# Two attentions in a row: the first one's weights are divided by their sums before they are transposed

## The chip, the core and the metric

The kernel runs on one NeuronCore of a Trainium2 chip, as one launch. Its time is the device time of one execution in microseconds (us). Every kernel is executed several times; the median is given with the lowest and the highest run. One execution is also recorded by the hardware profiler: it has a time of its own, and a span, from its first recorded instruction to its last.

## The reference

Two layers of attention stand behind each other: batch 8, 576 rows, 8 heads of width 64 first, and then 4 experts with one causal head of width 64 each, of which each row takes the best two.

```python
scores = scale * q @ k.T                                # first attention, per batch and head: 576 x 576
scores = np.where(scores >= max(scores) - tau, scores, -1e9)
a = exp(scores - max(scores)); a /= a.sum() + 1e-9
x = a @ v                                               # heads side by side: 576 x 512
for e in range(4):                                      # second attention, causal
    q, k, v = x @ wq[e], x @ wk[e], x @ wv[e]
    s = where(causal, -1e9, scale * q @ k.T)
    p = exp(s - max(s)); p /= p.sum() + 1e-9
    out += gate[e] * (p @ v @ wo[e])                    # the gate is a softmax over the best two
```

## The kernel before

The 64 (batch, head) pairs are worked as 32 pairs of heads, `n` = 0 to 31, four to a batch. Each pair's 576 query rows are cut into four tiles of 128 rows and a tail of 64. `scores(n, s)` (lines 331 to 361) makes one tile `s`: the matmuls of queries and keys, split in a high and a low part, go to PSUM (L1087 for every matmul); DVE copies the scores to SBUF and takes their minimum (they are negated) in one instruction (`s_min`, L1177); ACT takes the exponential (`s_exp`, L1190); DVE compares the scores with the threshold, multiplies the exponentials with the outcome and sums each row (`s_stt`, L1194: the threshold product of the text below). There are two such rows of 576 per tile, one per head, and one for the tail, where both heads share the 128 partitions: 288 for the whole kernel. TensorE then transposes the weights (`tr_pp`, L1239), and ACT or DVE evacuates them to `pa` and `pt` (L1063, L1065).

`attnv(n, tiles)` (lines 363 to 393) multiplies the transposed weights with `v`, in two groups of tiles per pair, 64 in all. The weights are not normalised at that point. The row sums were collected in a buffer `sg`; `g_sum` adds the epsilon (L1058), `g_inv` inverts (L1202), `g_wide` and `g_tail` spread each inverse over 64 columns in `iw` (on POOL L1067, on ACT L1063, on DVE L1065), TensorE transposes `iw` (`tr_inv`, by the helper at L1077), ACT or DVE evacuates that to `iv`, and DVE multiplies it with the product that lies in PSUM (`x_mul`, L1277; `x_tail`, L1281). `x_hi` and `x_lo` split the outcome in two parts for the second attention, which begins with projections that read `x`.

`second(b)` (from line 415) is the second attention of one batch. It divides its weights by their sums before their transposes: `add_eps` (L1058), `inv` (L1230), `share` for the gate (L1235) and `scale2` (L1492 on POOL and DVE, L1490 on ACT).

Two tables write the order out by hand. `ORDER` gives each task a place in one long list, `BY` gives its engine where it has a choice, and `plan` (from line 157) walks the list and gives out the buffers: eight `e` buffers for scores and weights, eight banks of PSUM, in pairs for transposes (class `d`) and scores (class `s`). Each engine runs its instructions in the order of the list and waits by semaphores for what the others make; TensorE has no choice of engine, and what comes next on it is what the list says.

```python
def evac(n, fn, deps, takes=(), uses=(), name="", engs=("ACT", "DVE")):   # out of PSUM
def small(fn, deps, sm, name):                                            # DVE, ACT or POOL
def scale2(self, e, sm, p2, w, j):
    p, x = self.row(p2)[:, :w], self.small(sm)[:, 10 + j:11 + j]
```

Of the kernel before, what the change touches and what calls it, by code (L numbers as in the profile page):

```python
# [246 lines left out]
def work(K):  # L247
# [47 lines left out]
    LD, PREP, PTS, VMB, X, AV, SUMS = {}, {}, {}, {}, {}, {}, {}  # L295
# [1288 lines left out]
```

## Time and profile before

| | |
|---|---|
| median of 3 runs | 832.75 us (831.75 to 833.85) |
| the profiled execution | 832.69 us, span 831.0 us |
| TensorE (PE), weight loads (PEld) | 808.6 us busy, 763.1 us busy |
| VectorE (DVE) | 733.6 us busy |
| ScalarE (ACT) | 653.5 us busy |
| GpSimd (POOL) | 280.9 us busy |

The busy time of an engine is the time in which at least one of its instructions runs; a line's share of it is counted so that overlapped time isn't counted twice. A matmul's end is modelled, so a busy PE need not work at its peak pace. "Idle before" is time for which an engine stood still ahead of a group's instructions, with what ended most of it. A line number can be that of a helper, so that the names of the tiles (out<-in) tell which step it is: `ps<-ident,iw` is the transpose of the inverse sums, `ps<-ident,e` at L1239 that of the first attention's weights.

### The profile page before, as it was taken

The page shows a single profiled execution, that of the slowest core. Times are in us where ns is not written, and L with a number is a line of the kernel's source. Part 1 is how long each engine was busy: PE and PEld are TensorE (multiplying, and loading weights), DVE is VectorE, ACT ScalarE, POOL GpSimd, SP SyncE. Part 2 cuts the span into 40 slices and gives each one's busy share as a digit, 9 for nine tenths or more (in the row PEclk, how much of TensorE's full clock was granted, in tenths as well). Part 3 has the DMA queues.
Part 4 walks back from the last instruction along what each step waited for, and adds up shares of the span by engine and source line. Part 5 has one row for each costly group of instructions (what it writes and reads, how often), then busy time and mean ns, then how long its engine had stood idle before and what let it go on. Part 6 is the DMA issues. An engine that isn't in the chain of part 4 may idle for free.

```text
span 831.0 us, 35075 instructions
## 1 busy us (share of the span) xinstructions
PE 808.6 (97%) x14472; PEld 763.1 (92%) x14472; DVE 733.6 (88%) x2327; ACT 653.5 (79%) x1374; POOL 280.9 (34%) x604
## 2 busy tenths in 40 slices
PE   9989999999999999999999999999999999989998
PEld 7888999999989998899999999989998899988997
DVE  6999999998899889899988999998999988889474
ACT  4999779976898679887689767898679877779465
POOL 5756504412332124521235231521133422231451
PEclk9999999999999999999999999999999999999999
DMA  4433212122121212122112321113022113110002
GB/s 108 97 85 79 51 35 47 32 61 50 30 69 44 79 44 46 33 52 46 30 44 63 90 70 30 39 32 97 22 60 60 27 55 76 33 40 3 15 27 78
DMA packets 135632, 43.18 MB, mean 52 GB/s; under 512 B 130608, under 2 KB 130608, under 8 KB 135472
## 3 DMA queue, kind: packets, MB, share of 16 engines
q1 hardware_dynamic: 134240, 40.64, 20.1%
q8 instruction: 114, 1.87, 1.0%
q10 hardware_dynamic: 1232, 0.30, 0.2%
q14 instruction: 46, 0.38, 0.2%
HBM read 31.47 MB, written 9.44 MB: 49 GB/s over the span
## 4 chain that ended last, share of the span: by engine, by line
PE 75%; DVE 14%; ACT 7%; issue 3%; SPq 1%; DMA 1%; POOL 0%; DVEq 0%; ACTq 0%; POOLq 0%
PE ps L1087 61%; PE ps L1239 7%; PE ps L1077 6%; DVE e L1194 4%; DVE e L1177 4%; ACT pt L1063 2%; ACT e L1190 1%; DVE e L1464 1%; ACT e L1469 1%; SPq L1090 1%; DVE kk L1134 1%; DVE iv L1277 1%; ACT pa L1063 1%; DMA qi<-in_q_dram 0%; DVE pt L1065 0%
## 5 line engine op out<-in xcount | busy, mean ns | idle before, releaser
L1190 ACT ACTIVATE e<-e,sm 128x576 f32<-128x576 f32 x288 | 214.4, 770 | 24.0 <-DVE e L1177 23.2
L1177 DVE TENSOR_SCALAR_CACHE_REDUCE e<-ps 128x576 f32<-128x576 f32 x288 | 209.5, 752 | 21.4 <-PE ps L1087 16.6
L1194 DVE SCALAR_TENSOR_TENSOR e<-e,sm,e 128x576 f32<-128x576 f32 x256 | 204.7, 818 | 4.3 <-ACT e L1190 2.6
L1087 PE MATMUL ps<-kk,qq 64*128 64x288 f32 x1920 | 175.4, 306 | 3.1 <-DVE e L1177 1.8
L1063 ACT ACTIVATE pt<-ps 128x640 f32<-128x640 f32 (+3 forms) x234 | 146.5, 644 | 27.1 <-PE ps L1239 19.0
L1087 PE MATMUL ps<-pt,vm 128*64 128x128 f32 (+1 forms) x1536 | 155.9, 258 | 0.0
L1087 PEld LDWEIGHTS ps<-kk,qq 64*128 64x128 f32 x1920 | 141.2, 186 | 9.0 <-DVE e L1177 3.5
L1087 PE MATMUL ps<-pa,vm 128*64 128x128 f32 x1024 | 135.8, 276 | 1.0 <-DVE kk L1134 0.5
L1087 PEld LDWEIGHTS ps<-pt,vm 128*64 128x64 f32 x1536 | 131.1, 137 | 0.0
L1239 PE MATMUL ps<-ident,e 64*128 64x64 f32 x2624 | 124.2, 226 | 4.9 <-DVE e L1177 2.3
L1239 PEld LDWEIGHTS ps<-ident,e 64*128 64x128 f32 x2624 | 107.8, 139 | 14.9 <-DVE e L1177 4.3
L1087 PEld LDWEIGHTS ps<-pa,vm 128*64 128x64 f32 x1024 | 111.9, 137 | 6.1 <-DVE kk L1134 0.7
L1087 PE MATMUL ps<-x,wh 64*128 64x288 f32 x1024 | 106.6, 296 | 0.3 <-ACT pa L1063 0.2
L1087 PEld LDWEIGHTS ps<-x,wh 64*128 64x128 f32 x1024 | 86.1, 185 | 1.1 <-DVE e L1177 0.4
L1063 ACT ACTIVATE pa<-ps 128x512 f32<-128x512 f32 x114 | 67.0, 594 | 21.7 <-PE ps L1239 18.8
L1087 PE MATMUL ps<-x,wl 64*128 64x288 f32 x512 | 80.2, 292 | 0.0
L1492 POOL TENSOR_SCALAR e<-e,sm 128x384 f32<-128x384 f32 (+4 forms) x104 | 62.0, 604 | 36.8 <-DVE sm L1235 23.6
L1469 ACT ACTIVATE e<-e,sm 128x128 f32<-128x128 f32 (+3 forms) x128 | 70.8, 556 | 3.2 <-DVE sm L1464 2.8
L1464 DVE CUSTOM_DVE_ANT_0 e<-ps,tri 128x128 f32<-128x128 f32 (+3 forms) x128 | 58.7, 484 | 5.2 <-PE ps L1087 4.6
L1087 PE MATMUL ps<-wh,x 64*128 64x260 f32 x576 | 60.8, 285 | 0.0
L1071 POOL TENSOR_TENSOR x<-iv,x 128x64 fp32r<-128x64 f32 (+2 forms) x67 | 44.8, 678 | 41.9 <-ACT x L1063 27.9
L1087 PE MATMUL ps<-pt,vt 128*64 128x128 f32 (+1 forms) x640 | 58.9, 262 | 0.0
(163 smaller groups left out, 1650.2 us busy)
## 6 DMA issues: line engine op xcount, KB each, us to landing
vm<-in_v_dram SPq DMA_DIRECT2D x64, 128.0 KB, 2.6
out_dram<-ob SPq DMA_DIRECT2D x32, 256.0 KB, 2.4
ki<-in_k_dram SPq DMA_DIRECT2D x96, 64.0 KB, 2.4
qi<-in_q_dram SPq DMA_DIRECT2D x62, 80.0 KB, 2.4
ki<-in_k_dram SPq DMA_DIRECT2D x32, 80.0 KB, 2.5
vt<-in_v_dram SPq DMA_DIRECT2D x128, 16.0 KB, 2.1
qi<-in_q_dram SPq DMA_DIRECT2D x31, 64.0 KB, 2.3
qi<-in_q_dram SPq DMA_DIRECT2D x31, 48.0 KB, 2.5
```

Source lines behind the costliest of these rows:

```text
L1063: self.nc.scalar.activation(dst, src, AF.Copy)
L1071: eng.tensor_tensor(dst, a, b.bitcast(F32), op=ALU.subtract)
L1077: self.nc.tensor.transpose(self.ps[:, bank, c * n:(c + 1) * n], x[sl], self.ident[sl, sl])
L1087: return self.nc.tensor.matmul(out, x, y, start=first, stop=last)
L1090: (self.nc.sync if e == "SP" else self.nc.scalar).dma_start(dst, src)
L1177: self.nc.vector.tensor_scalar(self.sides(sc), self.dbank(s)[:, :, :HS], 0.0, None, op0=ALU.add, op1=ALU.min, accum_out=self.small(sm)[:, ...
L1190: self.nc.scalar.activation(self.row(e), self.row(sc), AF.Exp, bias=self.small(sm)[:, 2 * j:2 * j + 1], scale=-1.0)
L1194: self.nc.vector.scalar_tensor_tensor(self.row(e), self.row(sc), self.small(sm)[:, 8 + j:9 + j], self.row(e), op0=ALU.is_le, op1=ALU.mult, ...
L1239: self.nc.tensor.transpose(self.ps[:, g.slot + h, c * D:(c + 1) * D], x, self.ident[sl, sl])
L1464: self.nc.vector.tensor_tensor_reduce(self.row(p2)[:, :w], self.dbank(g)[:, j, :w], self.tri[:, SM - w:], 1.0, FAR, op0=ALU.add, op1=ALU.m ...
L1469: self.nc.scalar.activation(p, p, AF.Exp, bias=m[:, 2 * j:2 * j + 1], scale=-1.0, accum_out=m[:, 4 + 2 * j:5 + 2 * j])
L1492: (self.nc.vector if e == "DVE" else self.nc.gpsimd).tensor_scalar(p, p, x, 0.0, op0=ALU.mult, op1=ALU.add)
```

## The change

The row sums of the first attention stay beside the other small numbers of a tile (`sm`) and `sg`, `iw` and all that was made of them go. Behind the threshold products of a tile there are now one addition of the epsilon (`plus`, 160 of them, on DVE, ACT or POOL), one inverse (`inv`, 160, DVE) and one scaling of each row of weights in place (`scale2`, 288, on POOL, DVE or ACT), and only then the transposes. Behind the product with `v`, a plain copy out of PSUM (`x_raw`, ACT or DVE, 64) takes the place of the two products. The order tables were written anew for the new list of tasks.

```diff
-        sg, done = SUMS[n, group(s)]
-        takes = [*bufs, *dict.fromkeys((sc, ee)), sm, sg]
+        takes = [*bufs, *dict.fromkeys((sc, ee)), sm]
...
+        a = small(lambda e: K.plus(e, sm, 10, 4, nj), xs, sm, f"eps1.{n}.{s}")
+        r = task("DVE", SMALL, lambda: K.inv(sm, nj), [a], [], [sm], name=f"rec1.{n}.{s}")
+        ns = [scaling(S, lambda e, j=j: K.scale2(e, sm, ees[j], S, j), r, sm, ee, f"pn.{n}.{s}") for j in range(nj)]
-            t = pe(nc * TR + TX, lambda j=j, g=g, nc=nc: K.tr_pp(g, ees[j], nc, s < R), xs if j == nj - 1 else [x], [g, pt], [ee], "R", ld=76.0, kind="T", name=f"tm.{n}.{s}")
+            t = pe(nc * TR + TX, lambda j=j, g=g, nc=nc: K.tr_pp(g, ees[j], nc, s < R), ns if j == nj - 1 else ns[:1], [g, pt], [ee], "R", ld=76.0, kind="T", name=f"tm.{n}.{s}")
...
-        a = task("DVE", SMALL, lambda: K.g_sum(sg, nt + nm), done, [], [sg], name=f"sum.{n}.{first}")
-        r = task("DVE", SMALL, lambda: K.g_inv(sg, nt + nm), [a], [], [sg], name=f"inv.{n}.{first}")
-        u = [moved(nm * P, lambda e: K.g_wide(e, sg, iw, nm), [r], [iw], [sg, iw], name=f"iw.{n}.{first}")]
-        if tail:
-            u.append(moved(P, lambda e: K.g_tail(e, sg, iw, nm), [r], [iw], [sg, iw], name=f"iw.{n}.{first}"))
-        t = pe(nt * TR + TX, lambda: K.tr_inv(gi, iw, nt), u, [gi, iv], [iw], "R", ld=76.0, kind="T", name=f"ti.{n}.{first}")
-        i = evac(nt * P, lambda e: K.iv_out(e, iv, gi, nt), [t], [], [gi, iv], name=f"iv.{n}.{first}")
-        l = task("DVE", t_dve(w), lambda: K.x_mul(g, iv, w), [av, i], [], [g, iv], name=f"xm.{n}.{first}")
-        if tail:
-            l = task("DVE", t_dve(ST + 100), lambda: K.x_tail(g, iv, w), [l], [], [g, iv], name=f"xm.{n}.{first}")
+        l = evac(w, lambda e: K.x_raw(e, g, iv, w), [av], [iv], [g, iv], name=f"xr.{n}.{first}")
...
+    def scaling(w, fn, r, sm, buf, name):
+        x = task(None, {"POOL": (270 + 0.84 * w, 30), "DVE": (215 + 0.515 * w, 80), "ACT": (285 + 0.84 * w, 101)}, fn, [r], [], [sm, buf], name=name)
...
+    "eps1": "1222220222020002110020212212212222222020010101021212202121001222010222222222200001222020020200220000012101202022222021202020001022002120022120011222221220101200",
+    "pn": "202200220202020020201220002000220022120202011002020020022020000020000000220012110200022022122000000020000002002222002120002000200002000000200002000002002200220011202000002222020020020202220002002122000000000002200002000022202220020000002000000020002022020102220201020220100000000102000022",
```

In the table `eps1` the digits stand for DVE, ACT and POOL: 54, 28 and 78 of the additions. In `pn` they stand for POOL, DVE and ACT: 174, 16 and 98 of the scalings. Of the 64 copies of `x_raw` ACT has 45 and DVE 19.

On PE, in the middle of the program, these are the rows from the keys' transposes of one pair of heads on (`ki`: keys, `qi`: queries, `e`: weights, `kk` with `qq`: scores, `iw`: spread inverses), before:

```order
L1077 MATMUL ps<-ident,ki_76 128x64 x10
L1239 MATMUL ps<-ident,e_435_6630 128x64 x10
L1087 MATMUL ps<-kk_421_6347,qq_428_6509 128x288 x12
L1077 MATMUL ps<-ident,iw_464_7019 128x64 x6
L1077 MATMUL ps<-ident,qi_77 128x64 x10
L1087 MATMUL ps<-k_419_6283,q_415_6250 128x256 x6
```

and in the changed kernel, from the same transposes on:

```order
L1068 MATMUL ps<-ident,ki_76 128x64 x10
L1205 MATMUL ps<-ident,e_402_6428 128x64 x8
L1205 MATMUL ps<-ident,e_408_6592 128x64 x10
L1205 MATMUL ps<-ident,e_425_6840 128x64 x10
L1078 MATMUL ps<-kk_399_6369,qq_407_6572 128x288 x12
L1205 MATMUL ps<-ident,e_425_6840 128x64 x8
L1078 MATMUL ps<-k_412_6658,q2d_89 128x288 x6
```

The group `ps<-ident,iw` that stood between the scores and the queries' transposes has gone, and transposes and scores follow each other directly; at this place the scores stand somewhat further on.

On ACT, in the opening, these rows stand ahead of the second batch of head pairs before (`e<-e,sm` at L1190: exponentials; `iw`, `iv`: the inverses; `wh`: a weight of the second attention):

```order
L1190 ACTIVATE e_54_838<-e_54_838,sm 128x576
L1190 ACTIVATE e_72_1038<-e_64_941,sm 128x576
L1190 ACTIVATE e_74_1073<-e_71_1020,sm 128x576
L1063 ACTIVATE iw_75_1075<-sg 128x256
L1190 ACTIVATE e_72_1038<-e_64_941,sm 128x576
L1190 ACTIVATE e_76_1085<-e_73_1040,sm 128x576 x2
L1190 ACTIVATE e_74_1073<-e_71_1020,sm 128x576
L1124 ACTIVATE pt_77_1140<-ps,qsc 128x640
L1063 ACTIVATE iv_79_1146<-ps 128x256
```

and in the changed kernel at about the same place (L1181: exponentials; L1452: scalings; L1054: copies):

```order
L1181 ACTIVATE e_67_1059<-e_59_943,sm 128x576 x2
L1181 ACTIVATE e_69_1101<-e_66_1030,sm 128x576
L1452 ACTIVATE e_57_911<-e_57_911,sm 128x576
L1452 ACTIVATE e_51_866<-e_51_866,sm 128x576
L1181 ACTIVATE e_70_1111<-e_68_1064,sm 128x576
L1181 ACTIVATE e_69_1101<-e_66_1030,sm 128x576
L1452 ACTIVATE e_57_911<-e_57_911,sm 128x576
L1181 ACTIVATE e_70_1111<-e_68_1064,sm 128x576
L1054 ACTIVATE iv_72_1147<-ps 128x320
```

Three scalings stand between the exponentials now, and the copies of `iw` are gone.

## Rows read from the trace of the kernel before

**Rows 1.** The page, part 1: busy us (share of the span), instructions.

```profile
PE 808.6 (97%) x14472; PEld 763.1 (92%) x14472; DVE 733.6 (88%) x2327; ACT 653.5 (79%) x1374; POOL 280.9 (34%) x604
```

**Rows 2.** Stretches: busy us (x instructions) of PE, PEld, DVE, ACT, POOL; clock.

```profile
20.00:100.00 80.00, 75.21 (x1364) 69.63 (x1362) 76.64 (x223) 71.43 (x132) 48.42 (x78) 1.00 0.37 82
100.00:700.00 600.00, 591.63 (x10754) 561.46 (x10752) 549.84 (x1740) 482.12 (x1014) 180.26 (x402) 1.00 0.21 50
```

**Rows 3.** Chain of waits by line, from 20 to 60 us, then 300 to 340 us.

```profile
by line: DVE e L1194 14.1%; DVE e L1177 13.8%; SPq L1090 12.7%; issue 9.0%; PE ps L1087 8.1%; ACT pt L1063 8.0%; ACT e L1190 7.2%; DMA ob<-in_moe_wk_dram 6.9%; PE ps L1239 6.0%; PE ps L1077 5.6%; ACT iw L1063 3.2%; ACT pt L1124 2.0%; DVE wl
...
by line: PE ps L1087 73.4%; PE ps L1239 10.2%; PE ps L1077 7.7%; DVE kk L1134 2.1%; DVE kk L1126 2.0%; DVE e L1177 1.9%; POOL fencePOOL L1353 1.9%; issue 1.1%; DVE sg L1202 0.2%
```

**Rows 4.** Lines of PE, PEld; columns: busy us, mean ns | idle before.

```profile
L1239 PE MATMUL ps<-ident,e 64*128 64x64 f32 x2624 | 124.2, 226 | 4.9 <-DVE e L1177 2.3 <-ACT pt L1063 0.8 <-DVE sg L1058 0.4
...
L1077 PE MATMUL ps<-ident,iw 64*128 64x64 f32 x320 | 22.7, 230 | 0.3 <-DVE e L1177 0.3
...
L1077 PEld LDWEIGHTS ps<-ident,iw 64*128 64x128 f32 x320 | 17.7, 138 | 3.0 <-issue 1.1 <-DVE e L1177 0.5 <-POOL e L1492 0.3
```

**Rows 5.** Instructions on iw by stretch; columns as in rows 2.

```profile
20.00:100.00 80.00, 3.08 (x45) 2.56 (x46) 0.00 (x0) 3.00 (x9) 2.78 (x5) 1.00 0.37 82
100.00:700.00 600.00, 16.91 (x240) 12.90 (x238) 1.54 (x6) 10.81 (x29) 13.55 (x37) 1.00 0.21 50
```

**Rows 6.** Lines of DVE.

```profile
L1194 DVE SCALAR_TENSOR_TENSOR e<-e,sm,e 128x576 f32<-128x576 f32 x256 | 204.7, 818 | 4.3 <-ACT e L1190 2.6
...
L1277 DVE TENSOR_TENSOR iv<-ps,iv 128x320 f32<-128x320 f32 (+1 forms) x64 | 29.0, 454 | 8.1 <-PE ps L1087 5.0 <-ACT iv L1063 0.9 <-issue 0.8
...
L1058 DVE TENSOR_REDUCE sm<-sm 128x2 f32<-128x4 f32 (+1 forms) x145 | 21.3, 150 | 3.8 <-ACT e L1469 2.3 <-ACT e L1484 0.4
...
L1230 DVE RECIPROCAL sm<-sm 128x2 f32<-128x2 f32 (+1 forms) x80 | 12.4, 159 | 1.1
...
L1202 DVE RECIPROCAL sg<-sg 128x5 f32<-128x5 f32 (+1 forms) x64 | 11.2, 177 | 0.6
...
L1058 DVE TENSOR_REDUCE sg<-sg 128x5 f32<-128x10 f32 (+1 forms) x64 | 10.0, 156 | 0.7
...
L1281 DVE TENSOR_TENSOR iv<-ps,iv 64x64 f32<-64x64 f32 x32 | 7.3, 228 | 1.0
```

**Rows 7.** Lines of ACT by shape, one of DVE, and ACT on iw.

```profile
L1063 ACT ACTIVATE iv<-ps 128x384 f32<-128x384 f32 x28 | 13.7, 489 | 6.7 <-PE ps L1077 6.6
...
L1063 ACT ACTIVATE iv<-ps 128x256 f32<-128x256 f32 x25 | 9.5, 378 | 5.2 <-PE ps L1077 4.5 <-PE ps L1239 0.6
...
L1185 ACT ACTIVATE sm<-sm 128x2 f32<-128x2 f32 x26 | 7.5, 290 | 2.7 <-DVE e L1177 2.4
...
L1490 ACT ACTIVATE e<-e,sm 128x576 f32<-128x576 f32 x2 | 1.6, 776 | 1.2 <-POOL sm L1235 0.6 <-DVE sm L1235 0.5
...
L1492 DVE TENSOR_SCALAR e<-e,sm 128x576 f32<-128x576 f32 x1 | 0.5, 512 | 0.0
...
L1063 ACT ACTIVATE iw<-sg 128x256 f32<-128x256 f32 (+1 forms) x42 | 15.2, 370 | 2.4 <-DVE sg L1202 1.8 <-ACT e L1190 0.5
```

**Rows 8.** Tile e: ns min/median/max, first to last start, shapes.

```profile
L1194 DVE SCALAR_TENSOR_TENSOR e<-e,sm,e x256: 770/812/1399, 18.7 to 768.5; 128x576 f32<-128x576 f32 x128
...
L1492 POOL TENSOR_SCALAR e<-e,sm x104: 370/592/1360, 136.5 to 817.0; 128x512 f32<-128x512 f32 x28, 128x384 f32<-128x384 f32 x24, 128x256 f32<-128x256 f32 x21, 128x128 f32<-128x128 f32 x18
```

**Rows 9.** Lines of POOL: the 128x576 scaling, then two with shapes together.

```profile
L1492 POOL TENSOR_SCALAR e<-e,sm 128x576 f32<-128x576 f32 x13 | 10.4, 797 | 8.3 <-DVE sg L1058 7.1 <-DVE sm L1235 0.5 <-PE ps L1239 0.3
...
L1187 POOL TENSOR_TENSOR sm<-sm 128x2 f32<-128x2 f32 (+1 forms) x64 | 20.9, 328 | 56.9 <-DVE e L1177 43.3 <-DVE sg L1058 8.0 <-DVE sm L1058 2.5
L1067 POOL TENSOR_SCALAR iw<-sg 128x256 f32<-128x256 f32 (+1 forms) x47 | 18.3, 393 | 73.3 <-DVE sg L1202 60.1 <-DVE sm L1058 6.1 <-PE ps L1087 4.9
```

**Rows 10.** PE weight loads' waits: us in total, times, longest us.

```profile
PEld ps L1077 <- POOL e L1492: 1.2, 4, 0.4
```

**Rows 11.** Second attention's first reads of tile x (same columns).

```profile
L1087 PEld LDWEIGHTS ps<-x,wh x1024: 182/185/195, 85.8 to 800.1; 64*128 64x128 f32 x171
```

More of the change, by code (lines that the diff above doesn't have):

```diff
@@ L288, in small @@
         return task(None, {"DVE": SMALL, "ACT": (288, 101), "POOL": (197, 30)}, fn, deps, [], [sm], name=name)
+    def scaling(w, fn, r, sm, buf, name):
+        x = task(None, {"POOL": (270 + 0.84 * w, 30), "DVE": (215 + 0.515 * w, 80), "ACT": (285 + 0.84 * w, 101)}, fn, [r], [], [sm, buf], name=name)
+        x.port = True
+        return x
     f32r = lambda n, w: n * max(110.0, w / 2.286 + 6)
@@ L293, in work @@
     LO = ("POOL", "DVE")
[L295 removed]
+    LD, PREP, PTS, VMB, X, AV = {}, {}, {}, {}, {}, {}
     TAU, WT, TRI = [], [], []
@@ L480, in score @@
             r = task(None, {"DVE": SMALL, "POOL": (197, 30)}, lambda e: K.share(e, sm, gw, t, ep, nj), [r, *gd], [], [sm, gw], name=f"shr.{name}")
-            ns = [task(None, {"POOL": (270 + 0.84 * w, 30), "DVE": (215 + 0.515 * w, 80), "ACT": (285 + 0.84 * w, 101)}, lambda e, j=j: K.scale2(e, sm, p2[j], w, j), [r], [], [sm, pb], name=f"p2s.{name}")
-                  for j in range(nj)]
-            for x in ns:
-                x.port = True
+            ns = [scaling(w, lambda e, j=j: K.scale2(e, sm, p2[j], w, j), r, sm, pb, f"p2s.{name}") for j in range(nj)]
             return p2, ns
@@ new lines @@
+    "xr": "0001011001010000011010000001100000010000011100000001000011100010",
+    "xh": "0110201100000012000112100002010011010110100001021002100001201101",
+    "xl": "1010010110010011000100000000001000000000000000110000100000001101",
+    "xd": "00000010100000000000111100001000",
+    "kr": "00100",
+    "qr": "00000",
+    "fpj": "02202001221010021222101121122220",
+    "qu": "00000011001000000001000100001001",
+    "qd": "02102100010001002000201010001110",
+    "fv": "0110122020211112",
+    "v2": "0000000001000110",
@@ L944 @@
+    "ob": "000001001000000100000001010100100000",
 }
@@ L1178, in s_min, with plus @@
                                      accum_out=self.small(sm)[:, 2 * j:2 * j + 1])
-    def s_thr(self, e, sm, js):
-        m, j, n = self.small(sm), js[0], len(js)
+    def plus(self, e, sm, to, of, n):
+        m = self.small(sm)
         if e == "DVE":
-            self.pairs(m, 8 + j, 2 * j, n)
+            self.pairs(m, to, of, n)
         elif e == "ACT":
-            self.nc.scalar.activation(m[:, 8 + j:8 + j + n], m[:, 2 * j:2 * (j + n):2], AF.Identity, bias=m[:, 1:2], scale=1.0)
+            self.nc.scalar.activation(m[:, to:to + n], m[:, of:of + 2 * n:2], AF.Identity, bias=m[:, of + 1:of + 2], scale=1.0)
@@ L1197, in g_sum @@
-    def g_sum(self, sg, n):
-        self.pairs(self.sgs[:, sg.slot], 12, 0, n)
-    def g_inv(self, sg, n):
-        x = self.sgs[:, sg.slot, 12:12 + n]
-        self.nc.vector.reciprocal(x, x)
-    def iw(self, buf):
-        return self.t(buf, [P, 3, P])
-    def g_wide(self, e, sg, iw, n):
-        t = self.iw(iw)[:, :n].rearrange("p t (j d) -> p (t j) d", j=2)
-        self.copy(e, t, self.sgs[:, sg.slot, 12:12 + 2 * n].unsqueeze(2).to_broadcast([P, 2 * n, D]))
-    def g_tail(self, e, sg, iw, n):
-        self.copy(e, self.iw(iw)[:, n], self.sgs[:, sg.slot, 12 + 2 * n:13 + 2 * n].to_broadcast([P, P]))
@@ L1215, in tr_inv, with s_stt @@
-    def tr_inv(self, g, iw, n):
-        for c in range(n):
-            self.transpose(g, c, self.iw(iw)[:, c])
+    def s_stt(self, sc, sm, e, j):
+        m = self.small(sm)
+        self.nc.vector.scalar_tensor_tensor(self.row(e), self.row(sc), m[:, 8 + j:9 + j], self.row(e), op0=ALU.is_le,
+                                            op1=ALU.mult, accum_out=m[:, 4 + 2 * j:5 + 2 * j])
     def iv(self, buf):
-        return self.t(buf, [P, 3 * P])
-    def iv_out(self, e, iv, g, n):
-        self.copy(e, self.whole(self.iv(iv)[:, :n * P]), self.halves(g, n))
+        return self.t(buf, [P, 2 * P + ST])
@@ L1274, in x_of, with x_raw @@
         return self.x(buf)[:, i * (S + ST):][:, :S]
-    def x_mul(self, g, iv, w):
-        self.nc.vector.tensor_tensor(self.iv(iv)[:, :w], self.bank(g)[:, :w], self.iv(iv)[:, :w], op=ALU.mult)
-    def x_tail(self, g, iv, w):
-        self.nc.vector.tensor_tensor(self.iv(iv)[D:, w - ST:w], self.bank(g)[D:, w - ST:w], self.iv(iv)[D:, w:w + ST], op=ALU.mult)
+    def x_raw(self, e, g, iv, w):
+        self.copy(e, self.iv(iv)[:, :w], self.bank(g)[:, :w])
     def x_hi(self, e, x, cols, iv, w):
```

220 lines of the change are left out of this document (92 added, 128 removed), and 295 rows, old and new, of tables (ORDER, SLOTS).

## The prediction

> **What bounds the kernel now.** First the engines' shares [rows 1]: TensorE (PE) is busy 808.6 of 831.0 us, VectorE (DVE) 733.6, ScalarE (ACT) 653.5, GpSimd (POOL) 280.9. Since a share is a mean over stages, the stretches come next [rows 2]. From 100 to 700 us PE works 591.6 of 600 us at the full granted clock (1.00, the 2.4 GHz level); DVE has 549.8, ACT 482.1. From 20 to 100 us it is otherwise: DVE 76.6 and ACT 71.4 of 80, PE 75.2. The chains of waits agree [rows 3]: between 300 and 340 us matmul lines carry 91% of the chain (73.4 + 10.2 + 7.7), between 20 and 60 us the first two entries are DVE's, 27.9%, and the PE lines that are listed carry some 20%. So **in the opening the elementwise engines set the pace, behind it PE does**, and an edit that takes work from PE and gives work to the others must be priced in each stage apart.
>
> **The change, part by part.**
>
> *PE loses the transposes of the inverse sums*: 320 instructions, 64 groups. What they cost has three rows [rows 4]: their own busy time is 22.7 us (71 ns each); at the 47 ns of the long transpose runs (124.2 us / 2624) they would cost 15.0 us; their weight loads are 17.7 us. The groups are short and stand between other transposes, so the true cost lies between; I take 17.7 us, and 15.0 and 22.7 are the ends. By stage [rows 5] 2.6 us of the 17.7 lie in the opening, where PE isn't the bound: 17.7 - 2.6 = **15.1 us gained** (ends 12.8 and 19.6, each with the opening's share taken off).
>
> *DVE*: gone are 64 sums at 156 ns, 64 inverses at 177, 64 products at 454 and 32 tail products at 228 [rows 6], 10.0 + 11.2 + 29.0 + 7.3 = 57.5 us, and 7 of the spread copies, 1.8 us. New are 160 inverses at 159 ns (25.4 us), 54 of the 160 additions of the epsilon at 150 ns (8.1), 16 scalings of 128x576 at 512 ns (8.2) and 19 copies of the raw product where 11 copies of the inverses were, 8 x 0.46 = 3.7. 45.4 - 59.3 = -13.9: DVE goes to about 720 us. This pays nothing by itself where PE is the bound.
>
> *ACT*: 98 scalings at 776 ns are 76.0 us, 28 additions at 290 ns 8.1 us; 42 spread copies, 15.2 us, go; 53 evacuations of inverses (13.7 + 9.5 = 23.2 us) become 45 of raw products, about 24 x 0.434 (between the rows of 384 and 256 elements) + 21 x 0.378 = 18.4 [rows 7]. Sum +64 us: ACT goes to about 718. Spread over the 768 us in which the first attention runs [rows 8], that is 482 + 64 x 600/768 = 532 of 600 us in the middle or, with the stretch shorter by PE's gain, 90%: still below PE, as DVE is today. In the opening it is not covered. Up to the 45th exponential, ACT's order holds 137 instructions before and 140 now: 19 scalings are new (14.7 us); gone are 9 spread copies at 370 ns (3.3), 3 evacuations of inverses (about 1.4) and, on balance, 4 other copies (some 1.7 at the 434 ns above). 71.4 + 8.3 = 79.7 of 80 us, beside a DVE that stays within 2 us of its 76.6. An engine that is needed for all of a stretch cannot hide its own waits, and ACT has them today: 80 - 71.4 = 8.6 us idle. I charge **+3 us** for the opening: the ends are 0 (the waits vanish, since work is always there) and 8 (they stay whole).
>
> *POOL*: 174 scalings at 797 ns are 138.7 us, 78 additions at 328 ns 25.6, less 47 spread copies (18.3) [rows 9]: 281 + 146 = 427 us, 52%. There is room, in the opening too (48.4 of 80, and the opening holds 45 of the 320 inverse transposes [rows 5], so about 146 x 45/320 = 21 us of the new work).
>
> *The new wait*: the transposes of the weights, which stood right behind the threshold product on DVE, now stand behind addition, inverse and scaling: 0.33 + 0.16 + 0.80 = 1.3 us later on POOL. Where another tile's work lies ready for PE this costs nothing; that cover is written into PE's order, where other tiles' transposes, scores and projections stand between a tile's scores and its transposes. If it's short, PE stands still. The nearest row is the same step in the second attention, where PE waited for POOL's scalings 1.2 us in 4 cases of 104 [rows 10]; 174 more at that rate are **+2.0 us**. The ends are 0 and 1.3 us for each of 32 head pairs' first tile, 42.
>
> *The end*: behind the last head pair nothing but the last batch is left, and the longer path to its transposes may show: +1.3 us, less 0.3 because the last product, 454 + 228 ns, becomes one copy of about 430 ns. **+1.0** (ends 0 and 1.3). Memory frees up too: the inverses' 64 double banks of PSUM are no longer asked for. PE's waits for banks have no row of their own; I price it at 0, and its cover is that PE idles 1.4% from 100 to 700 us, 8.4 us, which is the most it could give.
>
> The sum: -15.1 + 3.0 + 2.0 + 1.0 = -9.1 us. The profiled execution took 832.69 us (831.0 of span), the median of the runs is 832.75, so both lead to **823.6 us**.
>
> **A row and a rule.** POOL and DVE already get in each other's way here: the threshold product has a median of 812 ns, but a longest of 1399, and POOL's scaling a median of 592 and a longest of 1360 [rows 8]. On DVE it costs little: 256 x (818 - 812) ns = 1.5 us in all [rows 6, 8]. In the Trainium skill, "SBUF — State Buffer", section "SBUF: two separate sides", a Vector instruction with two SBUF inputs and a GpSimd instruction that reads SBUF take one pair of ports in turn: whichever starts first holds it for its whole length, and the other stands still. By that rule every scaling on POOL that meets a threshold product, and the reverse, would wait up to the other's whole length, and the third rival below, at 838 to 854 us, would be the likely one; by the row alone the order keeps most of them apart, and the sum above stands. So far the trace bears the rule out in the longest values and not in the medians.
>
> **The rivals.**
> 1. *PE gains all of it.* The transposes cost 22.7 us, the opening runs on DVE as before, and the freed banks give some of the 8.4 us: 832.7 - 19.6 - 4 = about 809 us. For it: PE's 98.6% in the middle. Against: ACT's 64 us more.
> 2. *Nothing moves*, 832.7 us: ACT, now as loaded as DVE, returns PSUM banks later, and PE waits for them as long as it saved. For it: three engines near 90% leave little play; ACT's evacuations already end 0.8 of the 4.9 us for which PE idles before the weights' transposes [rows 4]; and the weight loads are busy 763.1 of 831.0 us, 92% [rows 1], so PE has some play of its own. Against: in the opening PE holds 94% beside engines at 96 and 89%. The Trainium skill, "Perfetto Trace Analysis", section "Identifying the Most-Contended Engine", says that matmul busy time is a poor measure of how near TensorE is to its limit and that the busy share of weight loads is a good one, which would make this rival weigh more; no run here shows yet which of the two tells it better.
> 3. *Slower: PE waits for scaled weights.* The scaling on POOL meets threshold products (205 us of DVE in the larger of their two forms) and its own neighbours; 160 tiles have one or two scalings each. If a tile's transposes come late by 0.2 us on average, PE loses 32 us, and the time is 823.6 - 2 + 32 = about 854; at 0.1 us about 838. It decides from 0.07 us a tile (11 us), where the gain is gone. For it: scalings of up to 1360 ns, and POOL from 34 to 52%. Against: other tiles' work on PE, and 98 scalings that ACT takes, where no threshold product stands in the way.
>
> **How the numbers follow.** A measurement tells about 0.3% (2.5 us) from no change. The forecast (812 to 830 us) gets 0.56, rival 1 (below 812) 0.10, rival 2 (830 to 835) 0.14, rival 3 (above 835) 0.20. Faster by over 0.3% is the forecast and rival 1, **0.66**; the same **0.14**; slower **0.20**. The range leaves out half of rival 3's and most of rival 1's tail: **809 to 840 us**, which also takes in the ends of the PE term and of the opening.
>
> **What would show it.** Right: no inverse transposes on PE, PE below 795 us busy; ACT near 718, DVE near 720, POOL near 427; the 100-to-700 stretch's share of PE still above 97%; the opening (up to the first projection of the second attention) no shorter than today's 85.8 us [rows 11] and up to 3 us longer. The middle is wrong if PE's idle time before the weights' transposes, now 4.9 us [rows 4], grows beyond 10 us behind POOL or ACT (rival 3), or if PE waits mostly for ACT's evacuations (rival 2). The opening is wrong if it grows by more than 8 us. The port term is wrong if the mean of POOL's 128x576 scaling passes 1.0 us, or that of the threshold product 0.9 us.

## The result and the profile after

The changed kernel takes 822.59 us (median of 4 runs, 822.03 to 822.96) against 833.30 us of the kernel before beside it (831.75 to 834.32): a ratio of 0.987 [0.986, 0.989], 10.7 us less. Forecast were 823.6 us. The sum was 1 us off; whether its terms were right is another question, and most of what follows is about that.

The page of the changed kernel, part 1, answers [rows 1]:

```profile
PE 794.9 (97%) x14156; PEld 750.5 (91%) x14156; DVE 723.2 (88%) x2312; ACT 695.7 (85%) x1430; POOL 438.6 (53%) x850
```

PE is busy 13.7 us less, DVE 10.4 less, ACT 42 and POOL 158 us more. The stretches of the changed kernel, in the columns of [rows 2]:

```profile
20.00:100.00 80.00, 71.23 (x1266) 65.00 (x1263) 77.50 (x226) 74.56 (x125) 72.07 (x106) 1.00 0.35 77
100.00:700.00 600.00, 591.08 (x10672) 561.41 (x10669) 544.04 (x1744) 520.82 (x1082) 304.35 (x597) 1.00 0.21 51
```

In the opening PE has fallen from 94 to 89% and DVE is at 97%: PE waits more there. In the middle PE works 98.5% of the time, as before. The chain of waits of the changed kernel from 300 to 340 us is less PE's alone than in [rows 3]: the three PE lines carry 63%, where they carried 91, and products, minima and a scaling come in between. This window holds other work in the two kernels; over the whole stretch from 100 to 700 us PE's lines carry 81% before and 78% after.

```profile
by line: PE ps L1078 51.8%; PE ps L1205 8.0%; DVE e L1185 7.8%; issue 7.7%; DVE e L1168 5.7%; POOL e L1454 3.7%; PE ps L1068 3.3%; DVE e L1426 3.2%; DVE fenceDVE L1315 1.5%; DVE v L1369 1.2%; POOL ob L1407 1.0%; POOL ob L1409 0.9%; POOL ob 
```

The lines of the changed kernel that answer to [rows 4, 6, 7, 9]: the weights' transposes on PE, the threshold product on DVE, the scalings on ACT and POOL.

```profile
L1205 PE MATMUL ps<-ident,e 64*128 64x64 f32 x2624 | 124.2, 226 | 6.6 <-DVE e L1168 3.3 <-ACT pt L1054 1.0 <-POOL e L1454 0.5
...
L1185 DVE SCALAR_TENSOR_TENSOR e<-e,sm,e 128x576 f32<-128x576 f32 x256 | 207.3, 831 | 4.9 <-ACT e L1181 2.1 <-POOL sm L1178 0.9
...
L1452 ACT ACTIVATE e<-e,sm 128x576 f32<-128x576 f32 x100 | 75.7, 769 | 4.9 <-DVE sm L1196 4.8
...
L1454 POOL TENSOR_SCALAR e<-e,sm 128x576 f32<-128x576 f32 x188 | 144.4, 774 | 63.0 <-DVE sm L1196 50.7 <-ACT pt L1054 3.5 <-DVE sm L1201 2.4
```

PE's idle time before the weights' transposes went from 4.9 to 6.6 us, far from the 10 that would have spoken for the third rival. The threshold product has a mean of 831 ns (818 before), the scaling on POOL 774. Tile x in the changed kernel, as in [rows 11]: the first projection of the second attention comes at 89.7 us, 3.9 later than before.

```profile
L1078 PEld LDWEIGHTS ps<-x,wh x1024: 182/185/195, 89.7 to 789.9; 64*128 64x128 f32 x171
```

**A ruler for all kernels.** The second attention begins each of its eight batches with a block of 128 matmuls of `x` and `wh`. Sorted by start, the 1st, the 769th and the 897th of the 1024 are the beginnings of batches 1, 7 and 8. They cut the span into four lengths: the opening (start to batch 1), the middle (batch 1 to 7), the last pairs of the first attention (batch 7 to 8) and the rest. In us, from each kernel's profiled execution:

```
kernel              opening  middle  last pairs  rest   span
before                86.0   599.4     94.0      51.6   831.0
after                 89.7   591.7     87.8      51.7   820.9
r2_before_no_ti       86.0   600.1     94.2      51.6   831.9
r2c_before_no_ti      85.3   594.0     93.4      51.5   824.2
r9_before_short_mul   87.0   598.0     91.9      51.5   828.4
r1_pe_320             88.9   595.4     88.3      51.7   824.3
r1b_pe_640            89.0   601.2     89.0      51.8   831.0
r6_dve_back           91.2   616.5     94.8      51.7   854.2
r6b_dve_dose          90.2   595.3     89.2      51.7   826.4
r3b_open_no_scale     87.3   591.9     87.7      51.7   818.6
r5b_all_aside         89.9   591.3     87.7      51.8   820.7
r7_no_eps             94.1   597.2     88.4      51.7   831.4
r7c_no_eps_first      93.1   595.4     88.4      52.0   828.9
r7b_no_eps_second     89.1   591.4     87.8      51.7   820.0
```

So the change lost 3.7 us in the opening, won 7.7 in the middle and 6.2 in the last pairs, and nothing behind them. Each row comes from one execution, and the executions of the kernel before alone range from 830.2 to 835.1 us, so that 1 us more or less in one length says little.

But for what an experiment adds or leaves out, kernels of one order have the same work between two marks; the orders before and after do not quite. The middle and the last pairs, before and after (columns of [rows 2]):

```profile
86.00:685.40 599.40, 591.03 (x10755) 560.75 (x10754) 551.67 (x1741) 484.41 (x1015) 183.27 (x405) 1.00 0.20 50
685.40:779.40 94.00, 90.58 (x1622) 85.62 (x1618) 81.81 (x267) 74.04 (x164) 28.75 (x57) 0.98 0.14 34
...
89.70:681.40 591.70, 582.78 (x10527) 553.11 (x10527) 537.04 (x1723) 516.03 (x1067) 304.46 (x595) 1.00 0.21 51
681.40:769.20 87.80, 86.17 (x1573) 81.84 (x1570) 80.40 (x262) 76.96 (x164) 41.56 (x86) 1.00 0.13 29
```

Counted by their starts, 240 inverse transposes are gone from the middle and 40 from the last pairs, but the middle has only 230 matmuls less and the last pairs have 50 less: 12 matmuls of the output and 6 of the scores that stood in the last pairs stand in the middle in the new order, and 8 transposes of weights went the other way. At the mean busy time that their groups have in the kernel before, that is some 1.7 us of work moved (an estimate: 8 x 0.114 + 4 x 0.146 + 6 x 0.091 - 8 x 0.047). At equal work the middle has won some 9.4 us and the last pairs some 4.5.

### The profile page after: what moved, and what is told of

It is laid out like the page before. It is cut to its first block, busy times and chain, and to the rows that moved or that the text cites. A ratio compares the mean times of both kernels' runs of the same rounds, so it can differ in the third digit from the quotient of the medians.

```text
span 820.9 us, 34790 instructions
## 1 busy us (share of the span) xinstructions
PE 794.9 (97%) x14156; PEld 750.5 (91%) x14156; DVE 723.2 (88%) x2312; ACT 695.7 (85%) x1430; POOL 438.6 (53%) x850
## 4 chain that ended last, share of the span: by engine, by line
PE 69%; DVE 7%; ACT 4%; issue 2%; POOL 1%; DMA 1%; SPq 0%; DVEq 0%; ACTq 0%; POOLq 0%
PE ps L1078 57%; PE ps L1205 7%; PE ps L1068 4%; DVE e L1185 2%; DVE e L1168 2%; ACT pt L1054 1%; ACT e L1431 1%; ACT e L1181 1%; ACT e L1452 1%; DVE e L1426 1%; DMA vm<-in_v_dram 0%; DVE v L1369 0%; POOL e L1454 0%; ACT pa L1054 0%; DVE qq L1062 0%
## 5 line engine op out<-in xcount | busy, mean ns | idle before, releaser
L1454 POOL TENSOR_SCALAR e<-e,sm 128x576 f32<-128x576 f32 (+4 forms) x280 | 193.5, 700 | 71.4 <-DVE sm L1196 54.0
L1181 ACT ACTIVATE e<-e,sm 128x576 f32<-128x576 f32 x288 | 216.3, 771 | 15.6 <-DVE e L1168 11.8
L1185 DVE SCALAR_TENSOR_TENSOR e<-e,sm,e 128x576 f32<-128x576 f32 x256 | 207.3, 831 | 4.9 <-ACT e L1181 2.1
L1054 ACT ACTIVATE pt<-ps 128x640 f32<-128x640 f32 (+3 forms) x231 | 144.2, 642 | 13.6 <-PE ps L1205 6.9
L1178 POOL TENSOR_TENSOR sm<-sm 128x2 f32<-128x2 f32 (+1 forms) x142 | 42.3, 300 | 141.5 <-DVE e L1185 80.9
L1452 ACT ACTIVATE e<-e,sm 128x576 f32<-128x576 f32 (+4 forms) x131 | 91.9, 715 | 4.9 <-DVE sm L1196 4.8
L1431 ACT ACTIVATE e<-e,sm 128x256 f32<-128x256 f32 (+3 forms) x128 | 70.8, 556 | 1.4 <-DVE sm L1426 1.1
L1054 ACT ACTIVATE pa<-ps 128x512 f32<-128x512 f32 x108 | 63.3, 592 | 6.0 <-PE ps L1205 5.6
L1426 DVE CUSTOM_DVE_ANT_0 e<-ps,tri 128x384 f32<-128x384 f32 (+3 forms) x128 | 58.6, 484 | 3.6 <-PE ps L1078 2.0
```

The lines of the kernel that those rows point to most:

```text
L1054: self.nc.scalar.activation(dst, src, AF.Copy)
L1178: self.nc.gpsimd.tensor_tensor(m[:, to:to + n], m[:, of:of + 2 * n:2], m[:, of + 1:of + 2 * n:2], op=ALU.add)
L1181: self.nc.scalar.activation(self.row(e), self.row(sc), AF.Exp, bias=self.small(sm)[:, 2 * j:2 * j + 1], scale=-1.0)
L1185: self.nc.vector.scalar_tensor_tensor(self.row(e), self.row(sc), m[:, 8 + j:9 + j], self.row(e), op0=ALU.is_le, op1=ALU.mult, accum_out=m[ ...
L1426: self.nc.vector.tensor_tensor_reduce(self.row(p2)[:, :w], self.dbank(g)[:, j, :w], self.tri[:, SM - w:], 1.0, FAR, op0=ALU.add, op1=ALU.m ...
L1431: self.nc.scalar.activation(p, p, AF.Exp, bias=m[:, 2 * j:2 * j + 1], scale=-1.0, accum_out=m[:, 4 + 2 * j:5 + 2 * j])
```

## The experiments

All ratios are to the kernel before on the same chip (medians of 831.6, 832.5 and 832.1 us in the three groups in which the kernels ran). The changed kernel's 822.59 us stand beside a fourth median, 833.30 us, and the four differ by up to 1.7 us; a difference between its time and a time below is no surer than that.

### Are the transposes worth 15 us?

In the kernel before, the transposes of the inverses left out:

```diff
-        t = pe(nt * TR + TX, lambda: K.tr_inv(gi, iw, nt), u, [gi, iv], [iw], "R", ld=76.0, kind="T", name=f"ti.{n}.{first}")
+        t = pe(nt * TR + TX, lambda: K.iv_out(i.by, iv, iw, nt), u, [gi, iv], [iw], "R", ld=76.0, kind="T", name=f"ti.{n}.{first}")
-        i = evac(nt * P, lambda e: K.iv_out(e, iv, gi, nt), [t], [], [gi, iv], name=f"iv.{n}.{first}")
+        i = evac(nt * P, lambda e: None, [t], [], [gi, iv], name=f"iv.{n}.{first}")
...
+    def iv_out(self, e, iv, iw, n):
+        self.copy(e, self.iv(iv)[:, :n * P], self.iw(iw)[:, :n].rearrange("p t d -> p (t d)"))
```

> The kernel before, with its order and its buffers, without the 320 transposes of the inverse sums: the spread inverses are copied untransposed, so the products take wrong factors; nothing else is left out. Theory (behind the opening PE sets the pace, and the gain is these transposes): 15 us less than before, 817 to 821 us, with the opening unchanged at 86 us. Rival (the gain comes from the new order, the engines' new shares and DVE's lighter load): at most 4 us less, 829 to 833 us.

832.27 us, ratio 1.001 [1.000, 1.002]: nothing gained. But here the 64 copies had moved forward in the orders of ACT and DVE, to the place of the transposes, and waited there for the spread inverses. So the same again with the copies at their old place, reading a constant:

```diff
+        t = pe(nt * TR + TX, lambda: None, u, [gi, iv], [iw], "R", ld=76.0, kind="T", name=f"ti.{n}.{first}")
+        i = evac(nt * P, lambda e: K.iv_out(e, iv, nt), [t], [], [gi, iv], name=f"iv.{n}.{first}")
...
+    def iv_out(self, e, iv, n):
+        self.copy(e, self.iv(iv)[:, :n * P].rearrange("p (t d) -> p t d", d=P), self.ident.unsqueeze(1).to_broadcast([P, n, P]))
```

> Kernel before without its 320 transposes of the inverses, and nothing that waits for anything new: the spread copies are still made, and at the place of the old evacuations 64 copies of a constant of the same width fill the factor of the products (so x of the first attention is not divided by the right sums). Theory A (TensorE's own work is the pace behind the opening, as the prediction had it): 15 us of its work go, so 817 to 821 us. Theory B (VectorE's queue is the pace and TensorE has play): VectorE's work is as before, so 829 to 833 us. Theory C (each of several engines carries a share): 824 to 828 us.

826.24 us, ratio 0.993 [0.991, 0.996]: 6 us gained, 5.4 of them evenly along the middle. PE's busy time fell by 10.4 us, and its idle time (span less busy) rose from 22.4 to 26.0. So what is taken from PE in the middle does shorten it, but a transpose is worth 6.2 us / 320 = 19 ns, not the 47 to 71 ns at which the prediction priced it. Even that is not the transposes' work alone: the copies no longer wait for them either, for which ACT had waited 11.1 us in all in the kernel before. And the two kernels, 6 us apart, differ in nothing but where 64 copies stand, what they read and what they wait for; which of these it was stays open.

The other way round, transposes put back in the changed kernel, 320 and then 640 (repeats of ones that are made anyway):

```diff
-        for c in range(nc):
+        for c in [0] * (1 if j or not full else 0) + list(range(nc)):
```

> The changed kernel with 320 transposes more on PE: the first chunk of each of the 160 tiles' last weight transposes is done twice, in place, with no new buffer, wait or consumer. Theory: PE's own work sets the pace, so the 9.6 us (30 ns each at the pace of a long run) to 15.0 us (47 ns each by busy time), less the opening's share, come back: 831 to 836 us. Rival (PE's lost work was not what counted): at most 3 us more, 822 to 826 us.

> The same with 640 transposes more (the first chunk three times). Theory: twice the increase, 839 to 849 us, and the increase per transpose the same as with 320. Rival: at most 6 us more, or a bend (the second 320 cost much more than the first), which would say that PE has play today.

826.25 us, 0.993 [0.992, 0.995], and 832.78 us, 1.001 [1.000, 1.002]. The first 320 cost 3.7 us, the next 320 6.5; in the middle 3.7 and 5.8. That looks like a price that rises with the dose, as if PE had a little play first. But the first step is one of those between groups: by the ratios to the kernel before it is 5.1 us, and the second 6.8, so that the bend is likely and not certain. No wait and no other work was added here, so that 12 to 20 ns are the price of a transpose by itself, in a run of others. The Trainium skill, "Perfetto Trace Analysis", section "Identifying the Most-Contended Engine", calls matmul busy time a poor measure of how near TensorE is to its limit and the weight loads' share a better one. These runs fit that, as far as the bend holds: PE, at 97% by the one and 91% by the other, took the first dose at a lower price than the second.

### Does DVE's relief pay?

In the kernel before, the 64 products of DVE over 2 columns instead of 256 or 320; every wait stays:

```diff
-        self.nc.vector.tensor_tensor(self.iv(iv)[:, :w], self.bank(g)[:, :w], self.iv(iv)[:, :w], op=ALU.mult)
+        self.nc.vector.tensor_tensor(self.iv(iv)[:, :2], self.bank(g)[:, :2], self.iv(iv)[:, :2], op=ALU.mult)
```

> Kernel before, with each of VectorE's 64 products of the raw product and the inverses cut from 384 or 256 columns to 2 (the rest of x is left undivided and wrong); every instruction, wait and place stays, TensorE's work too. That takes some 0.3 us from each of 64 instructions, 19 us from VectorE. Theory A: within 3 us of before, 829 to 833 us. Theory B: most of the 19 us, so 814 to 821 us. Theory C: a part of it, 822 to 828 us.

830.30 us, ratio 0.998 [0.996, 0.999]. The product's mean fell from 454 to 155 ns, 19 us in all, and 2 us came of it. By the ruler they lie in the last pairs (94.0 to 91.9), but there it is the clock that differs, as shown further on. In the changed kernel, DVE loaded instead of relieved, first with reductions of the tile that was just copied:

```diff
         self.copy(e, self.iv(iv)[:, :w], self.bank(g)[:, :w])
+        self.x_again(iv, w)
+    def x_again(self, iv, w):
+        for i, n in enumerate((w, D)[:2 if w > 2 * P else 1]):
+            self.nc.vector.tensor_reduce(self.aside[:, i:i + 1], self.iv(iv)[:, :n], axis=AX.X, op=ALU.max)
```

> The changed kernel with the time of the old products put back on DVE alone: behind each of the 64 raw copies DVE reduces the copy over its 256 or 320 columns, and over 64 more for 32 of them, into a column that nobody reads; 64 x about 0.45 + 32 x about 0.22 = 36 us. Theory: DVE has 9% play behind the opening, so 31 of the 36 us cost at most 4 us, and the opening, where DVE has 3% play, takes its 5 us: 825 to 831 us. Rival (DVE is the bound and its 14 us less were the gain): 850 us and more.

856.33 us, ratio 1.030 [1.028, 1.031]. That was meant as a dose of work, but it added a wait too. The waits of DVE in this kernel (us in total, times, longest):

```profile
DVE aside L1249 <- ACT iv L1055: 20.4, 18, 2.1
```

All that stands behind such a reduction in DVE's order waits for ACT with it. The same kind of load on a constant waits for nothing:

```diff
+        self.nc.vector.tensor_reduce(self.aside[:, 0, :2], self.ident.unsqueeze(1).to_broadcast([P, 2, P]), axis=AX.X, op=ALU.max)
```

> Kernel after, with 64 reductions of a constant of 256 columns on VectorE, one behind the place of each raw product's copy, which wait for nothing and which nobody reads: some 64 x 0.35 = 22 us more for VectorE, and no new wait. Theory A (VectorE has play): 823 to 826 us. Theory B: 840 to 845 us. Theory C: 828 to 836 us.

828.28 us, ratio 0.996 [0.994, 0.997]. The added group, in the lines of DVE:

```profile
L1245 DVE TENSOR_REDUCE aside<-ident 128x2 f32<-128x256 f32 x64 | 26.2, 409 | 0.0
```

DVE's busy time rose by 16 us to 739.2 (the rest of the 26.2 overlaps other instructions of its own), and the span by 5.5. So DVE does not set the pace, and relief is worth little, but load is not free: about a third of a us for each us. Work on DVE cost 5.7 us where work and a wait together, with 33 us of reductions, cost 34, of which some 5 are clock (granted over the whole span: 0.994, and 1.00 in the other kernel).

### What do the new scalings and their wait cost?

Scalings of ACT and POOL written aside in the changed kernel, so that no transpose waits for one of them, and, in another kernel, none for the first five pairs:

```diff
-        ns = [scaling(S, lambda e, j=j: K.scale2(e, sm, ees[j], S, j), r, sm, ee, f"pn.{n}.{s}") for j in range(nj)]
+        ns = [scaling(S, lambda e, j=j: K.scale_aside(e, sm, ees[j], S, j), r, sm, ee, f"pn.{n}.{s}") for j in range(nj)]
...
+        ns = [scaling(S, lambda e, j=j: K.scale2(e, sm, ees[j], S, j) if n >= 5 else None, r, sm, ee, f"pn.{n}.{s}") for j in range(nj)]
```

> Kernel after, with every scaling of the first attention that ScalarE or GpSimd makes written aside to a tile nobody reads (those weights are transposed undivided, so x is wrong there); same work in the same places, but the transposes of the weights no longer stand behind the scaling. Theory 1, the prediction's: the new wait costs 2 us in all, so 820 to 823 us. Rival: the wait is what holds back TensorE's gain, so 812 to 818 us.

> Kernel after without the scalings of the first five head pairs (45 instructions of 576 columns fewer on ScalarE, GpSimd and VectorE; x of those pairs is left undivided); all else as in after. Theory 1, the prediction's: ScalarE's and the others' new work in the opening costs 3 to 4 us there, so the first projection comes at 85 to 87 us instead of 89.7, and the time is 817 to 820 us. Rival: the opening's loss comes from its order, so the first projection stays behind 88.5 us and the time is 821 to 823 us.

Written aside: 821.99 us, ratio 0.988 [0.987, 0.990], spans 820.7 against 820.9. The wait costs nothing that can be measured. It is there in the waits of PE's weight loads in the changed kernel:

```profile
PEld ps L1205 <- POOL e L1454: 2.8, 7, 0.5
```

but where it is taken away, something else ends last. Without scalings in the opening: 820.28 us, ratio 0.986 [0.984, 0.987]. The first projection of that kernel:

```profile
L1078 PEld LDWEIGHTS ps<-x,wh x1024: 182/185/195, 87.3 to 787.6; 64*128 64x128 f32 x171
```

So by these two executions 2.4 of the opening's 3.9 us are the scalings; 1.5 are not, and where these come from wasn't tried. The 2.4 may be too little: without the scalings the granted clock was 0.77 and 0.89 in the stretches from 25 and from 30 us, and 1.00 in the changed kernel. In the medians the gain is 2.3 us, by the ratios 1.2.

### Less work, more time

Each sum of weights holds a 1, so the epsilon changes no bit of it in fp32, and its additions can go:

```diff
-        a = small(lambda e: K.plus(e, sm, 10, 4, nj), xs, sm, f"eps1.{n}.{s}")
-        r = task("DVE", SMALL, lambda: K.inv(sm, nj), [a], [], [sm], name=f"rec1.{n}.{s}")
+        r = task("DVE", SMALL, lambda: K.inv(sm, nj), xs, [], [sm], name=f"rec1.{n}.{s}")
...
-            a = task("DVE", SMALL, lambda: K.add_eps(sm, nj), es, [], [sm], name=f"eps.{name}")
-            r = task("DVE", SMALL, lambda: K.inv(sm, nj), [a], [], [sm], name=f"rec.{name}")
+            r = task("DVE", SMALL, lambda: K.inv(sm, nj), es, [], [sm], name=f"rec.{name}")
```

> Kernel after without the additions of the epsilon in both attentions (each sum holds the largest weight, which is 1, so that 1e-9 changes no bit of it in fp32): 160 small instructions fewer in the first (54 of VectorE, 28 of ScalarE, 78 of GpSimd), 80 of VectorE fewer in the second, about 20 us of VectorE in all. TensorE's work stays. Theory A: 818 to 823 us. Theory B: 803 to 812 us. Theory C: 812 to 818 us.

832.14 us, ratio 1.000 [0.999, 1.001]: 240 instructions less, in the same order on PE, and all of the change's gain was gone. The plan also gave some tiles other buffers, so the two halves were run apart, with plan and buffers as in the changed kernel (the tasks stay in the list and issue nothing, and the inverse reads the sums):

```diff
-        a = small(lambda e: K.plus(e, sm, 10, 4, nj), xs, sm, f"eps1.{n}.{s}")
+        a = small(lambda e: None, xs, sm, f"eps1.{n}.{s}")
...
-            a = task("DVE", SMALL, lambda: K.add_eps(sm, nj), es, [], [sm], name=f"eps.{name}")
+            a = task("DVE", SMALL, lambda: None, es, [], [sm], name=f"eps.{name}")
```

> Kernel after, its second attention inverting the sums without adding the epsilon (which changes no bit of a sum of at least 1 in fp32): 80 reductions of VectorE fewer, some 12 us, with buffers, places and order as in after. Theory A (TensorE's work alone is the pace): 821 to 823 us. Theory C (VectorE carries a share of 0.15 to 0.35): 818 to 821 us. Theory B (VectorE is the pace): 810 to 813 us.

> Kernel after, its first attention inverting the sums without adding the epsilon (54 small instructions of VectorE, 28 of ScalarE, 78 of GpSimd fewer), with buffers, places and order as in after. If the time that the kernel without any epsilon lost came from GpSimd's scalings that now meet VectorE's threshold products: those products' mean goes from 831 to over 850 ns and the time is 826 to 834 us. If it came from the other buffers that its plan chose: the mean stays near 831 ns and the time is 815 to 822 us.

The second attention's: 821.63 us, ratio 0.988 [0.986, 0.989], the lowest median of a kernel that computes everything, but not to be told from the changed kernel's 0.987. DVE has 6.7 us less to do, and the middle is 0.3 us shorter. The first attention's: 829.95 us, ratio 0.997 [0.996, 0.998], 7.4 us more than the changed kernel. By the ruler 3.4 are lost in the opening and 3.7 in the middle, bit by bit from batch to batch. The loss in the opening has one place. DVE in this kernel's timeline (start us, us, line, operation):

```profile
45.98 0.75 DVE L1168 TENSOR_SCALAR_CACHE_REDUCE e<-ps 128x576 f32<-128x576 f32 x1
...
46.65 5.51 DVE L1185 SCALAR_TENSOR_TENSOR e<-e,sm,e 128x576 f32<-128x576 f32 x1
...
52.10 0.81 DVE L1185 SCALAR_TENSOR_TENSOR e<-e,sm,e 128x576 f32<-128x576 f32 x1
```

and POOL:

```profile
46.09 0.72 POOL L1058 TENSOR_SCALAR kk<-pt 128x640 fp32r<-128x640 f32 x1
46.78 0.40 POOL L1058 TENSOR_SCALAR wh<-ob 128x256 fp32r<-128x256 f32 x1
47.15 0.40 POOL L1272 TENSOR_SCALAR ob<-ob 128x256 f32<-128x256 f32 x1
47.52 0.87 POOL L1062 TENSOR_TENSOR kk<-pt,kk 128x320 fp32r<-128x320 f32 x1
48.35 0.74 POOL L1062 TENSOR_TENSOR wl<-ob,wh 128x256 fp32r<-128x256 f32 x1
49.05 0.86 POOL L1062 TENSOR_TENSOR kk<-pt,kk 128x320 fp32r<-128x320 f32 x1
49.87 1.67 POOL L1062 TENSOR_TENSOR qq<-pt,qq 128x320 fp32r<-128x320 f32 x2
54.41 0.19 POOL L1178 TENSOR_TENSOR sm<-sm 128x2 f32<-128x2 f32 x1 [2.86 <-DVE sm L1200]
```

A threshold product of 0.8 us lasted 5.51. It started while POOL worked, and POOL had seven more instructions ready without a pause; the product ended 0.6 us behind the last of them. No wait of DVE is recorded there, so that POOL held it up is read from the times. The kernel without any epsilon has a product of 5.52 us at the same place; no other product in the 14 kernels lasted over 1.5 us. PE then waited 4.3 us in one piece for the minimum behind the product, and came back at a lower clock, as this kernel's stretches show (granted clock in the third column from the end):

```profile
45.00:50.00 5.00, 3.89 (x68) 3.17 (x63) 5.00 (x7) 4.96 (x9) 5.00 (x9) 1.00 0.22 48
50.00:55.00 5.00, 1.29 (x12) 1.29 (x14) 5.00 (x12) 0.64 (x1) 1.89 (x4) 0.72 0.47 107
55.00:60.00 5.00, 5.00 (x60) 5.00 (x58) 5.00 (x16) 4.13 (x7) 1.66 (x2) 0.59 0.00 1
60.00:65.00 5.00, 4.82 (x106) 4.53 (x102) 2.24 (x8) 3.38 (x6) 2.59 (x6) 1.00 0.09 22
```

0.59 stands between full speed (2.4 GHz) and half of it (1.2 GHz). In the Trainium skill, "SBUF — State Buffer", section "SBUF: two separate sides", a Vector instruction with two SBUF inputs and a GpSimd instruction that reads SBUF exclude each other from a pair of ports, and whichever starts first holds it for its whole length. The trace fits that one stands still for the other, and goes further: here the waiting side was passed over seven times. It need not be: in the changed kernel POOL has the same run of instructions, two products go through between them, and POOL waits in its turn, 0.95 and 0.90 us where it took 0.40:

```profile
47.92 0.81 DVE L1185 SCALAR_TENSOR_TENSOR e<-e,sm,e 128x576 f32<-128x576 f32 x1
...
48.66 0.94 DVE L1185 SCALAR_TENSOR_TENSOR e<-e,sm,e 128x576 f32<-128x576 f32 x1
...
48.05 0.95 POOL L1058 TENSOR_SCALAR wh<-ob 128x256 fp32r<-128x256 f32 x1
48.97 0.90 POOL L1268 TENSOR_SCALAR ob<-ob 128x256 f32<-128x256 f32 x1
```

What decides between the two courses is not shown. The mean of the 256 products rose to 870 ns in this kernel, 10 us in all, of which 4.7 are this one product; the expectation that was bound to this, 826 to 834 us and over 850 ns, held. The kernel without any epsilon takes some 3 us more than its two halves together (829.95 + 821.63 - 822.59 = 829.0); its other buffers may be the cause, which wasn't tried.

## Why the prediction was right, and where it wasn't

**The sum** was right to 1 us by luck, because errors cancelled. By the spans, PE's transposes were priced some 9 us too high (15.1 for the 6.0 us that they are worth in the middle and the last pairs), the three losses some 2 too high (6.0 for 3.8), and some 8 us were won that no term names.

**PE's term failed in its size**: "15.1 us gained". The runs show 6 us for the same 320 transposes taken from the kernel before, 3.7 us for 320 put into the changed one and 6.5 for 320 more. The mechanism stood in part: behind the opening the time follows what PE has to do, in both directions, but at a fraction of the busy time, and with the copies at another place the same transposes were worth nothing. The step that was wrong is the price. Both ends, 47 and 71 ns, were busy times, in which overlapping matmuls are told apart by modelled ends; PE's pace changes by 12 to 20 ns for such a transpose. Where they were taken out, the busy time fell by 33 ns each, not 55, and a third of that came back as idle time (22.4 to 26.0 us).

**DVE "pays nothing by itself where PE is the bound"** held nearly: 19 us less in DVE's products gave 2 us.

**The last pairs** won 6.2 us, where the prediction had only their share of the transposes. The kernel before, around 740 us:

```profile
735.00:740.00 5.00, 4.58 (x82) 4.21 (x82) 5.00 (x19) 4.65 (x11) 1.03 (x2) 1.00 0.41 93
740.00:745.00 5.00, 3.52 (x62) 2.92 (x59) 3.40 (x18) 3.37 (x10) 2.65 (x6) 0.95 0.22 69
745.00:750.00 5.00, 4.70 (x64) 4.50 (x62) 3.55 (x11) 4.01 (x12) 0.76 (x2) 0.71 0.00 0
750.00:755.00 5.00, 4.78 (x84) 4.40 (x83) 4.83 (x19) 4.93 (x15) 1.30 (x3) 1.00 0.01 3
```

PE stands still for 1.5 of 5 us, and its clock falls to 0.95 and 0.71 in this stretch and the next, which takes some 1.7 us from it ((0.05 + 0.29) x 5). What PE waits for is not DVE but ACT, which evacuates weights. From 735 to 752 us (us in total, times, longest):

```profile
PE ps L1087 <- ACT pa L1063: 1.8, 2, 1.4
```

With DVE's products cut, PE stands still there just as long, and that execution keeps its clock:

```profile
740.00:745.00 5.00, 3.54 (x57) 3.14 (x59) 3.24 (x18) 3.69 (x9) 3.40 (x8) 1.00 0.06 16
745.00:750.00 5.00, 4.50 (x72) 3.87 (x68) 4.93 (x17) 4.93 (x15) 0.00 (x0) 1.00 0.01 3
```

So of the 2.1 us by which its last pairs are shorter, some 1.7 are the clock of one execution. In the changed kernel PE stands still for 1.1 us, and the clock stays whole:

```profile
735.00:740.00 5.00, 3.92 (x71) 3.50 (x73) 4.59 (x21) 4.64 (x13) 3.90 (x10) 1.00 0.26 80
740.00:745.00 5.00, 4.74 (x72) 4.10 (x70) 4.64 (x18) 5.00 (x14) 4.80 (x10) 1.00 0.02 3
745.00:750.00 5.00, 4.96 (x104) 4.73 (x102) 5.00 (x18) 4.74 (x10) 1.98 (x6) 1.00 0.00 0
```

In the chain of waits from 700 to 780 us DVE's lines have 22% before, 14% with its products cut, and 5% in the changed kernel: DVE does stand in the way less often, but what that alone is worth wasn't tried. Before:

```profile
by line: PE ps L1087 46.2%; DVE e L1194 8.3%; DVE e L1177 7.7%; PE ps L1239 4.8%; PE ps L1077 3.9%; ACT e L1469 3.5%; issue 2.9%; DVE e L1464 2.3%; DVE iv L1277 2.2%; POOL e L1492 2.2%; DVE pt L1065 1.9%; ACT pt L1063 1.9%; ACT pa L1063 1.5
```

and after:

```profile
by line: PE ps L1078 68.9%; PE ps L1205 9.6%; PE ps L1068 5.1%; ACT pt L1054 3.4%; ACT e L1431 3.2%; DVE e L1185 1.8%; DVE e L1168 1.7%; ACT e L1181 1.7%; issue 1.0%; ACT e L1446 0.9%; DVE sm L1164 0.8%; DVE e L1426 0.5%; ACT z L1054 0.3%; 
```

Of the 6.2 us some 1.7 are this clock, 1.7 the work that the new order does earlier, 1.8 PE's idle time in this length (3.4 to 1.6 us), and 0.6 the transposes. That leaves little, but the cause of the shorter idle time wasn't tried: another order, no inverses on the way to `x`, fewer banks asked for. In the middle, of some 9.4 us at equal work, 5.4 are the transposes and up to 2 DVE's relief; the other 2 to 4 stay open.

**The opening**, +3.0, was +3.9, and the scalings are the larger part of it, as said. That ACT would be full was not: 74.6 of 80 us, not 79.7. POOL, DVE and ACT are now all at 90% or above there, and PE is the one that waits.

**The new wait**, +2.0, was 0 within the measurement. Of its ends, 0 and 42, the row of the second attention pointed to the right one. **The end**, +1.0, was +0.1: the rest behind batch 8's first projection is 51.6 and 51.7 us.

**Busy times**: DVE 723 (forecast 720), POOL 439 (427), ACT 696 (718). For ACT the groups were added up as if they didn't overlap, and DVE took over some of its copies. The 768 us over which the prediction spread ACT's work are 750 by [rows 8] (18.7 to 768.5), which changes its 532 us by one; measured were 521.

**The rivals.** That nothing moves was nearest to the truth in one thing, PE's play, with which the low price of the transposes fits. The third, PE waiting for scaled weights behind the port pair, didn't come: both means stayed below the 0.9 and 1.0 us that were named. But the kernel without the first attention's epsilon shows that it is close by: there one collision took back 3.4 us in the opening, and longer products, 5.3 us without that one, go with 3.7 us more in the middle.
